# Decode step of a small transformer block: the first twelve granules of each row laid out as closed 512 KiB blocks

## The chip, the cores and the metric

One core of one Trainium2 chip. The metric is the device time of one execution in microseconds, the median over several executions.

## The reference

The block is applied twice, with the same caches: attention of one new token over cached keys and values, then a small ReLU network, each with a residual. Sizes: batch 8, 32 heads of 128, 4096 cached positions, model width 640, hidden width 1728, all bf16.

```python
def _A_ref(x, k_cache, v_cache, wq, wo):            # B=8, Hq=Hkv=32, Sk=4096, Dh=128
    q = (x @ wq).reshape(B, 1, 32, 128).transpose(0, 2, 1, 3)
    p = softmax(einsum("bhqd,bhkd->bhqk", q, k_cache) * 128 ** -0.5)
    o = einsum("bhqk,bhkd->bhqd", p, v_cache)
    return o.transpose(0, 2, 1, 3).reshape(B, 1, 4096) @ wo
def _B_ref(x, w1, w2):
    return relu(x @ w1) @ w2
x = x + _A_ref(layernorm(x), k_cache, v_cache, wq, wo)
x = x + _B_ref(layernorm(x), w1, w2)
x = x + _A_ref(layernorm(x), k_cache, v_cache, wq, wo)
x = x + _B_ref(layernorm(x), w1, w2)
```

The caches are 512 MiB. They don't fit on the core, so most of them is read from DRAM twice, once for each application: of 2 x 1024 blocks of 512 KiB, 1856 are loaded.

## The kernel before

One batch entry is a "row". Its keys and values lie in DRAM as 128 partitions, each with 128 pieces of 4 KiB. Piece `p` of all 128 partitions is a **granule** of 512 KiB, the unit in which buffers are handed out. On the core there are 26 buffers of that size (`arena`). A host routine, `plan`, lays down the whole order of work in advance: it goes through the row for the first layer, then again for the second, with the next row woven in. To spare loads it keeps 24 granules of a row from its first pass to its second: `G - SPARE` = 21 stay in their buffers and three wait elsewhere on the core, mostly in PSUM (`STASH`). While they wait, only five buffers are left to work with. That is the **turn**: the end of a row's first pass and the start of its second.

```python
G = 26                # buffers of one granule
SPARE = 5             # of them free in a turn
STASH = 3
PAD = 2048            # elements after each partition's row: pitch 516 KiB, not 512
...
    first = [(which, hp, g) for which, hp in first for g in range(UNIT)]    # 24 granules
    keep = set(first[: G - SPARE])
    stash = first[G - SPARE : G - SPARE + STASH]
...
    def feed():                       # called whenever a buffer comes free
        while at[0] < len(stream):
            ...                       # most: how long a load may be now, least: how long it must be
            b, p = place(stream[at[0]])
            n = 1
            while n < most and place(stream[at[0] + n]) == (b, p + n):
                n += 1
            ...                       # u: the first of n free buffers in a row, or return
            ops.append(("load", b, p, n, u))
...
    def do_load(b, p, n, u):          # L637 of the profile
        nc.sync.dma_start(out=arena[:, u * GW : (u + n) * GW],
                          in_=A_kv[b, :, p * GW : (p + n) * GW])
...
    # host side
    kv = np.pad(kv.reshape(B, p, -1), ((0, 0), (0, 0), (0, PAD)))
```

A load takes one to eight granules. In the turns, where buffers come free one at a time, it mostly takes one. All loads are issued by SP, in order, and each waits until PE has done with the buffer that it fills.

Of the kernel before, what the change touches and what calls it, by code (L numbers as in the profile page):

```python
# [16 lines left out]
UNIT = 4  # L17
# [5 lines left out]
SOON = 4  # L23
PACE, LATE = 0.6, 2
PAD = 2048
AHEAD = 2
BANK = 512
CAP = 20
# [2 lines left out]
def tile_at(NP, which, hp):  # L31

    return max(0, 2 * hp - 1) if which == "K" else min(2 * hp + 2, 2 * NP - 1)


def plan(B, NP, n_up, n_down):
# [9 lines left out]
    for b in range(B - 1):  # L46
        nxt = [(0, b + 1, hp) for hp in order0]
        cur = [(1, b, hp) for hp in order1]
        if b + 1 < B - 1:
            visits += nxt[:AHEAD] + cur + nxt[AHEAD:]  # L50
        else:
            visits += nxt[:AHEAD] + cur[: NP - AHEAD] + nxt[AHEAD:] + cur[NP - AHEAD :]
    visits += [(1, B - 1, hp) for hp in order1]
    NV = len(visits)
    assert NV == 2 * B * NP and NP % GP == 0
    turns = [visits.index((1, b, order1[0])) for b in range(B)]
    moving = [not any(t - AHEAD - 1 <= i < t + 5 for t in turns) and i < NV - 2 for i in range(NV)]
    last_of = {(layer, b): v for v, (layer, b, hp) in enumerate(visits)}
    direct = [i == NV - 1 or visits[i][0] == 0 and last_of[visits[i][:2]] == i for i in range(NV)]
    ahead = [next((t - i for t in turns if 0 < t - i <= AHEAD), 0) for i in range(NV)]  # L60

# [13 lines left out]
    stream, uses = [], []  # L75
    for which, i in slots:
        layer, b, hp = visits[i]
# [18 lines left out]
    at = [0, 0]  # L96
    clock = [5.0, 6.0]

    def keeps(which, i, g):
        return visits[i][0] == 0 and (which, visits[i][2], g) in keep  # L100
# [6 lines left out]
    def place(x):  # L107

        return visits[x[1]][1], tile_at(NP, x[0], visits[x[1]][2]) * UNIT + x[2]

    def room(n):

        us = [u for u in range(G - n + 1) if not any(owner[u : u + n])]
        return min(us, key=lambda u: max(freed[u : u + n])) if us else None

    def feed():

        while at[0] < len(stream):
            lead = clock[1] - clock[0]
            calm = (PACE * (nth[stream[at[0]]] - at[1]) - LATE - lead) / 1.2  # L120
            least = next((n for us, n in LEADS if lead >= us), 1)
            least = min(least, max(1, (G - len(kept) - 2) // 3))
            most = min(max(least, int(calm)), LEADS[0][1], max(1, (len(stream) - at[0]) // 2))
            least = min(least, most)
            b, p = place(stream[at[0]])
            n = 1
            while n < most and place(stream[at[0] + n]) == (b, p + n):
                n += 1
            least = min(n, least)
            u = next((u for n in range(n, least - 1, -1) if (u := room(n)) is not None), None)  # L130
            if u is None:
                return
            n = next(k for k in range(n, 0, -1) if room(k) == u)
            for k, (which, i, g) in enumerate(stream[at[0] : at[0] + n]):
                ops.extend(("weights",) + w for w in weights.pop(i, []) if which == "K")
                owner[u + k] = True
                where[which, i, g] = u + k
                if keeps(which, i, g):
                    kept[which, b, visits[i][2], g] = u + k
            at[0] += n  # L140
            clock[1] = max(clock[1], clock[0] + 1.4) + 0.1 + 1.2 * n
            lands[u : u + n] = [clock[1] + 2] * n
            ops.append(("load", b, p, n, u))

    def find(which, i, g):
        u = where.get((which, i, g))
        return kept[which, visits[i][1], visits[i][2], g] if u is None else u
# [59 lines left out]
    def finish(layer, b):  # L207

        def own(n, *op):
            return n, ("C", layer, b, *op)  # L210

        c = []
        for k in range(n_up):
            c += [own(15, "up", k)]
            if layer:
                c += [own(0, "relu", k)]
            elif k == min(1, n_up - 1):
                c += [own(0, "var"), own(0, "root")]
        if layer:
            for k in range(n_up):  # L220
                c += [own(15, "down", k)] + [own(0, "var"), own(0, "root")] * (k == n_up // 2)
            return c + [own(0, "add")]
        c += [own(0, "relu")] + [own(14, "down", k) for k in range(n_down)] + [own(0, "add")]
        c += [own(2, "mean"), own(0, "center")] + query(b, 0)
        c += [own(1, "var2"), own(0, "root2")] + query(b, 1)
        return c

    feed()
    for which, i in slots:
        layer, b, hp = visits[i]  # L230
# [16 lines left out]
        for g in range(UNIT):  # L247
            u = find(which, i, g)
# [13 lines left out]
        else:  # L262
# [12 lines left out]
            if last_of[layer, b] == i and (layer == 0 or b == B - 1):  # L275
                chains[-1] += [(14, ("W", i)), (0, ("YC", i))] + finish(layer, b)
            elif layer == 0 or b == B - 1:
                chains[-1] += [(10, ("W", i)), (0, ("Y", i))]
                if last_of[layer, b] == next(v for v in range(i + 1, NV) if visits[v][:2] == (layer, b)):
# [17 lines left out]
def kernel(  # L297
    ctx: ExitStack,
    tc: tile.TileContext,
    A_x: bass.AP,  # L300
    A_kv: bass.AP,
    A_wq: bass.AP,
    A_wo: bass.AP,
# [6 lines left out]
    nc = tc.nc  # L310
    P = nc.NUM_PARTITIONS

    B, Sq, D = A_x.shape
    H = A_wo.shape[1] // D
    NP = H // 2
    Dh = A_kv.shape[1]
    W = (A_kv.shape[2] - PAD) // (2 * NP)
    Sk = W // 2
    Dff = B_w1.shape[1] // (D // P)
    assert Sq == 1 and Dh == P and D % P == 0 and W % (UNIT * P) == 0  # L320
    DC = D // P
    NJ = Sk // P
    GW = W // UNIT
    assert GW == 4 * BANK and Sk == UNIT * 2 * BANK
# [11 lines left out]
    kv = ctx.enter_context(tc.tile_pool(name="kv", bufs=1))  # L336
# [3 lines left out]
    arena = kv.tile([P, G * GW], BF16, name="arena")  # L340
# [25 lines left out]
    def load_weights(which, g=0):  # L366
# [15 lines left out]
        out=ident, in_=ident, pattern=[[-1, P]], compare_op=ALU.not_equal,  # L382
# [12 lines left out]
    for c in range(4):  # L395
        rows, at = slice(32 * c, 32 * c + CJ), c // 2 * 2 * CJ + c % 2
# [237 lines left out]
            copy(out=arena[:, u * GW + n * 2 * BANK : u * GW + (n + 1) * 2 * BANK], in_=t)  # L634

    def do_load(b, p, n, u):
        nc.sync.dma_start(out=arena[:, u * GW : (u + n) * GW], in_=A_kv[b, :, p * GW : (p + n) * GW])  # L637

    def do_q0(g):

# [32 lines left out]
    def do_mm(which, i, g, u):  # L673
# [19 lines left out]
        for c in range(4):  # L693
            if moving[i]:
# [5 lines left out]
                continue  # L700
            s_tiles[i] = o_ps[:, 2 * NJ : 4 * NJ] if ahead[i] == AHEAD else s_ps[:, i % 2 * 2 * NJ : (i % 2 + 1) * 2 * NJ]
            h = 2 * hp + c // 2
# [140 lines left out]
    def do_y(i):  # L843
# [3 lines left out]
        nc.vector.tensor_tensor(out=xT[:, b0 : b0 + nb, :], in0=xT[:, b0 : b0 + nb, :], in1=y, op=ALU.add)  # L847

    does = dict(WS=do_ws, S=do_s, SM=do_sm, SC=do_sc, YC=do_yc, load=do_load, stash=do_stash, unstash=do_unstash, weights=load_weights, mm=do_mm, M1=do_m1, T=do_t, M2=do_m2, B=do_b, E=do_e,
                L=do_l, I=do_i, OC=do_oc, OG=do_og, O=do_o, W=do_w, Y=do_y, C=do_finish, Q0=do_q0, Q=do_q, QC=take_q, QZ=do_qz, PT=do_pt, PC=do_pc, clear=do_clear)  # L850

# [15 lines left out]
def _laid_out(A_x, A_k_cache, A_v_cache, A_wq, A_wo, B_w1, B_w2):  # L867

    p = 128
    B, H, Sk, Dh = A_k_cache.shape  # L870
    D, HD = A_wq.shape
    Dff = B_w1.shape[1]
    NP, NJ, DC, NG, FC = H // 2, Sk // p, D // p, H // 2 // GP, -(-Dff // p)
    c = np.ascontiguousarray
    w2 = np.zeros((FC * p, D), B_w2.dtype)
    w2[:Dff] = B_w2
    k = A_k_cache.reshape(B, NP, 2, UNIT, Sk // UNIT, Dh).transpose(0, 1, 5, 3, 2, 4).reshape(B, NP, Dh, 2 * Sk)
    v = A_v_cache.reshape(B, NP, 2, UNIT, NJ // UNIT, p, Dh).transpose(0, 1, 5, 3, 2, 4, 6).reshape(B, NP, p, -1)
    kv = np.empty((B, p, 2 * NP, 2 * Sk), A_k_cache.dtype)
    for hp in range(NP):  # L880
        kv[:, :, tile_at(NP, "K", hp)] = k[:, hp]
        kv[:, :, tile_at(NP, "V", hp)] = v[:, hp]
    kv = np.pad(kv.reshape(B, p, -1), ((0, 0), (0, 0), (0, PAD)))
    return {
        "A_x": c(A_x),
        "A_kv": kv,
        "A_wq": c(A_wq.reshape(DC, p, NG, HD // NG).transpose(1, 2, 0, 3)).reshape(p, -1),
        "A_wo": c(A_wo.reshape(H, Dh, D).transpose(1, 0, 2)).reshape(Dh, -1),
        "B_w1": c(B_w1.reshape(DC, p, Dff).transpose(1, 0, 2)).reshape(p, -1),
        "B_w2": c(w2.reshape(FC, p, D).transpose(1, 0, 2)).reshape(p, -1),  # L890
    }
# [25 lines left out]
```

## Time and profile before

| | before |
|---|---|
| median of 3 runs | 2340.54 us (2339.28 to 2341.31) |
| profiled span | 2343.0 us |
| load queue, share of 16 DMA engines' span | 99.4% |
| PE busy | 60% |

In the profile, PE is the matrix engine (PEld its weight loads), DVE, ACT and POOL are the other compute engines, and SP is the engine that issues the loads. The page of the kernel before, by slices of the span (each 58.6 us), the count of packets, the load queue, and the chain that ended last by engine:

```profile
...
DMA  9999999999999999999999999999999999999997
GB/s 411 430 433 401 433 432 432 431 396 432 432 432 430 404 434 431 430 427 403 433 432 431 426 412 434 430 432 420 427 431 427 432 416 430 431 431 431 396 433 329
DMA packets 76753, 990.87 MB, mean 423 GB/s; under 512 B 8596, under 2 KB 8596, under 8 KB 36500
...
q1 hardware_dynamic: 76564, 988.12, 99.4%
...
DMA 71%; PE 17%; ACT 6%; DVE 3%; issue 2%; SPq 0%; POOL 0%; ACTq 0%; DVEq 0%; POOLq 0%
...
```

The load queue is busy for 99.4% of what sixteen engines have. The line GB/s is the rate in each slice: it holds near 430 and dips every fifth slice or so, down to 396. Those are the turns. The last line is the chain of waits: 71% of the span passes in waiting for a load. So a change has to pay through the load queue.

The loads of the kernel before, by size, with the median time from issue to landing:

```profile
...
issues: line engine op xcount, KB each, median us to landing
arena<-in_A_kv_dram SPq DMA_DIRECT2D x124, 4096.0 KB, 23.1
arena<-in_A_kv_dram SPq DMA_DIRECT2D x98, 2048.0 KB, 22.7
arena<-in_A_kv_dram SPq DMA_DIRECT2D x218, 512.0 KB, 6.5
...
```

Windows of the kernel before inside the first two turns. The last two columns are the DMA engines' busy share and the rate:

```profile
...
core 0: us, PE busy (x) PEld busy (x) DVE busy (x) ACT busy (x) POOL busy (x), PEclk, DMA share, GB/s
200.00:210.00 10.00, 8.44 (x227) 7.32 (x224) 2.95 (x18) 0.64 (x3) 2.33 (x11) 1.00 0.98 354
480.00:490.00 10.00, 7.76 (x214) 6.22 (x211) 3.19 (x20) 1.22 (x4) 0.56 (x3) 1.00 0.94 363
490.00:500.00 10.00, 8.15 (x177) 6.17 (x175) 1.71 (x10) 1.28 (x6) 1.78 (x8) 1.00 1.00 373
500.00:510.00 10.00, 8.07 (x173) 5.52 (x171) 2.82 (x18) 1.65 (x5) 2.54 (x12) 1.00 1.01 376
...
```

In the turn the engines are nearly as busy as elsewhere (0.94 to 1.01; a share over 1 comes from packets whose records overlap), but move 354 to 376 GB/s where they move about 430 elsewhere. So what they carry there takes longer.

What SP waited for before it issued a load, summed over the span (L637 is the load):

```profile
engine line waited for: us in total, times, longest us
SPq L637 <- DMA arena<-in_A_kv_dram: 836.5, 274, 13.2
SPq L637 <- PE small_ps L781: 301.9, 81, 7.5
SPq L637 <- PE s_ps L695: 290.0, 68, 9.5
SPq L637 <- PE o_ps L687: 261.9, 97, 7.9
SPq L637 <- PE small_ps L742: 101.4, 28, 6.0
...
```

SP waits both for PE, which frees buffers, and for loads, behind which PE stands.

The trace also has a record for each DMA packet, with its size, start and duration. One packet is one partition's run of a load, so a load of one granule has 128 packets of 4 KiB, eight on each engine. From these records of the kernel before I worked out:

```
packet size         4 KiB   8 KiB   16 KiB   32 KiB
packets             27904    6144    12544    15872
median, ns            159     309      611     1213
mean, ns            166.6   310.5    612.3   1215.2
excess per engine    13.3     0.6      1.0      2.2   us   (sum of duration less the median of its size, over 16)
```

(Packets of the load queue alone.) The medians are 150.5 ns per 4 KiB plus 8.5 ns per packet. **Excess** is used below for the last row: the time by which packets outlasted the usual time of their size. Over all sizes of the key and value loads it is 17.5 us. Of these, 13.3 are in the 4 KiB packets, and 10.7 of the 13.3 in the 156 single loads that start in the first twelve granules of a row. It isn't spread evenly: 735 of the 27904 packets of 4 KiB last over 200 ns, 444 ns on average, and these hold 13.1 of the 13.3 us.

### The profile page before, as it was taken

What the parts mean: (1) busy time and instruction counts of PE and PEld (TensorE: products, weight loads), DVE (VectorE), ACT (ScalarE), POOL (GpSimd) and SP (SyncE); (2) the same over time, 40 slices, a digit from 0 to 9 for tenths busy, and PEclk for the clock granted to TensorE, in tenths of its full rate; (3) what the DMA queues carried; (4) which work ended last, traced back from release to release, by engine and by line L of the source; (5) the groups of instructions that cost most, each with busy time, mean ns of one, the idle gap of its engine ahead of it and who ended that gap; (6) DMA issues with size and microseconds to landing.
All of it is one profiled execution on the core that took longest, in us unless ns stands there. A gap on an engine that the chain in (4) does not pass through costs nothing.

```text
span 2343.0 us, 43024 instructions
## 1 busy us (share of the span) xinstructions
PE 1398.6 (60%) x18748; PEld 591.4 (25%) x18748; DVE 496.7 (21%) x2022; ACT 426.3 (18%) x986; POOL 59.5 (3%) x296
## 2 busy tenths in 40 slices
PE   3547654576545764557545675556755567545766
PEld 1214211152111511125111241113411133111523
DVE  1113211131112211122111221112211122111312
ACT  1111211122111221112211121111211112111211
POOL 0000000000000000000000000000000000000000
PEclk9999999999999998555555555555555555555555
DMA  9999999999999999999999999999999999999997
GB/s 411 430 433 401 433 432 432 431 396 432 432 432 430 404 434 431 430 427 403 433 432 431 426 412 434 430 432 420 427 431 427 432 416 430 431 431 431 396 433 329
DMA packets 76753, 990.87 MB, mean 423 GB/s; under 512 B 8596, under 2 KB 8596, under 8 KB 36500
## 3 DMA queue, kind: packets, MB, share of 16 engines
q1 hardware_dynamic: 76564, 988.12, 99.4%
q8 instruction: 146, 2.39, 0.4%
q14 instruction: 43, 0.35, 0.0%
HBM read 988.08 MB, written 0.01 MB: 422 GB/s over the span
## 4 chain that ended last, share of the span: by engine, by line
DMA 71%; PE 17%; ACT 6%; DVE 3%; issue 2%; SPq 0%; POOL 0%; ACTq 0%; DVEq 0%; POOLq 0%
DMA arena<-in_A_kv_dram 71%; PE o_ps L687 5%; PE s_ps L695 4%; PE s_ps L705 2%; ACT P_row L755 2%; ACT o_sb L795 1%; PE small_ps L655 1%; DVE mrow L713 1%; ACT P_sb L761 1%; PE small_ps L800 1%; ACT arena L634 1%; PE small_ps L768 1%; PE small_ps L825 1%; DVE hmx L732 0%; ACT nmax L753 0%
## 5 line engine op out<-in xcount | busy, mean ns | idle before, releaser
L687 PE MATMUL o_ps<-arena,P_sb 128*4 128x512 bf16 x3952 | 584.3, 596 | 402.0 <-DMA arena<-in_A_kv_dram 401.0
L695 PE MATMUL s_ps<-arena,qz 128*4 128x512 bf16 x3040 | 410.3, 602 | 261.1 <-DMA arena<-in_A_kv_dram 249.5
L687 PEld LDWEIGHTS <-P_sb 128*4 128x4 bf16 x3952 | 107.4, 88 | 502.8 <-issue 491.7
L713 DVE TENSOR_REDUCE mrow<-s_ps 100x1 bf16<-100x512 f32 x190 | 131.8, 694 | 323.2 <-PE s_ps L695 323.2
L795 ACT CAST o_sb<-o_ps 100x512 bf16<-100x512 f32 x247 | 144.9, 587 | 289.3 <-PE o_ps L687 286.0
L753 ACT ACTIVATE nmax<-small_ps 100x1 f32<-100x1 f32 x106 | 18.1, 171 | 774.5 <-PE small_ps L742 774.5
L775 DVE CAST P_sb<-small_ps 128x64 bf16<-128x64 f32 x190 | 42.6, 224 | 523.1 <-PE small_ps L768 523.1
L695 PEld LDWEIGHTS <-qz 128*4 128x4 bf16 x3040 | 63.9, 85 | 313.7 <-issue 295.5
L705 PEld LDWEIGHTS <-arena 128*128 128x128 bf16 x4224 | 129.6, 104 | 40.8 <-DMA arena<-in_A_kv_dram 23.4
L705 PE MATMUL s_ps<-qo,arena 128*128 128x1 bf16 x3712 | 123.7, 165 | 17.2 <-ACT P_sb L761 7.6
L768 PE MATMUL small_ps<-few,P_row 100*128 100x16 bf16 x760 | 52.3, 179 | 92.1 <-ACT P_row L755 92.1
L753 ACT ACTIVATE nmax<-small_ps,q_scale 100x1 f32<-100x1 f32 x84 | 22.0, 261 | 398.7 <-PE small_ps L742 398.7
L787 DVE TENSOR_REDUCE lsum<-small_ps 128x2 f32<-128x64 f32 x240 | 53.9, 224 | 171.9 <-PE small_ps L781 171.9
L768 PEld LDWEIGHTS <-P_row 100*128 100x128 bf16 x760 | 35.0, 107 | 186.5 <-ACT P_row L755 178.2
L720 PE MATMUL small_ps<-few,mrow 100*1 100x16 bf16 x190 | 34.4, 181 | 67.6 <-DVE mrow L713 67.6
L755 ACT ACTIVATE P_row<-s_ps,nmax 100x512 bf16<-100x512 f32 x106 | 72.8, 687 | 3.4
L800 PEld LDWEIGHTS <-o_sb 100*128 100x128 bf16 x988 | 45.7, 106 | 107.2 <-ACT o_sb L795 73.8
L655 PE MATMUL small_ps<-xq,wq_sb 128*128 128x1 bf16 x1200 | 48.8, 165 | 38.9 <-DVE qo L812 33.5
L800 PE MATMUL small_ps<-few,o_sb 100*128 100x2 bf16 x988 | 65.1, 170 | 10.7 <-DVE lsum L787 2.2
L727 DVE TENSOR_REDUCE diag<-small_ps 1x2 bf16<-1x16 f32 x190 | 30.8, 162 | 186.9 <-PE small_ps L720 186.9
L720 PEld LDWEIGHTS <-mrow 100*1 100x1 bf16 x190 | 15.0, 79 | 210.8 <-DVE mrow L713 210.8
L755 ACT ACTIVATE P_row<-s_ps,nmax,q_scale 100x512 bf16<-100x512 f32 x84 | 65.3, 778 | 2.8
(225 smaller groups left out, 958.0 us busy)
## 6 DMA issues: line engine op xcount, KB each, us to landing
arena<-in_A_kv_dram SPq DMA_DIRECT2D x124, 4096.0 KB, 23.1
arena<-in_A_kv_dram SPq DMA_DIRECT2D x98, 2048.0 KB, 22.7
arena<-in_A_kv_dram SPq DMA_DIRECT2D x218, 512.0 KB, 6.5
arena<-in_A_kv_dram SPq DMA_DIRECT2D x48, 1024.0 KB, 11.3
arena<-in_A_kv_dram SPq DMA_DIRECT2D x11, 3072.0 KB, 22.4
arena<-in_A_kv_dram SPq DMA_DIRECT2D x11, 2560.0 KB, 20.5
arena<-in_A_kv_dram SPq DMA_DIRECT2D x10, 1536.0 KB, 19.7
wq_sb<-in_A_wq_dram SPq DMA_DIRECT2D x4, 1280.0 KB, 17.6
```

What stands on the lines that cost most here:

```text
L655: nc.tensor.matmul(q_ps[:, h : h + 1], lhsT=wq_sb[:, g, c, (2 * n + h) * Dh : (2 * n + h + 1) * Dh], rhs=xlns[b][:, 0, c : c + 1], start=( ...
L687: nc.tensor.matmul(o_ps[32 * c : 32 * c + CJ, :], lhsT=P_tiles[i][:, h, j : j + CJ], rhs=arena[:, at + c * CJ * Dh : at + (c + 1) * CJ * D ...
L695: nc.tensor.matmul(s_ps[32 * c : 32 * c + CJ, :], lhsT=qz[:, i % 3, c // 2, 3 - g : 3 - g + CJ], rhs=arena[:, at + c * BANK : at + (c + 1) ...
L705: nc.tensor.matmul(s_tiles[i][:, j : j + 1], lhsT=arena[:, at + n * P : at + (n + 1) * P], rhs=qo[:, b, h : h + 1], start=True, stop=True,)
L713: nc.vector.tensor_reduce(out=m_tiles[i][:OR, :1], in_=s_ps[:OR], axis=AX.X, op=ALU.max)
L720: nc.tensor.matmul(turn_ps[:1, : 4 * CJ], lhsT=m[:OR, :1], rhs=rsel[:OR], start=True, stop=True)
L755: nc.scalar.activation(out=P_rows[i][:OR], in_=s_ps[:OR], func=ACT.Exp, bias=nm[:OR, :1], scale=more)
L768: nc.tensor.matmul(P_ps[:, k * 4 * CJ : (k + 1) * 4 * CJ], lhsT=P_row[:OR, k * P : (k + 1) * P], rhs=rsel[:OR], start=True, stop=True,)
L775: nc.vector.tensor_copy(out=P_tiles[i].rearrange("p h (c k) -> p h c k", k=BANK // P), in_=P_ps.rearrange("p (k h c) -> p h c k", k=BANK / ...
L787: nc.vector.tensor_reduce(out=L, in_=(lsum2_ps if ahead[i] else lsum_ps).rearrange("p (h j) -> p h j", h=2), axis=AX.X, op=ALU.add)
L795: nc.scalar.copy(out=o_tiles[i][:OR], in_=o_ps[:OR, :].rearrange("p (j d) -> p j d", j=CJ))
L800: nc.tensor.matmul(oy[i][:, :2], lhsT=o_tiles[i][:OR, j, :], rhs=gsel[:OR, j, :], start=(j == 0), stop=(j == CJ - 1))
```

## The change

The intent: the single loads read 128 pieces of 4 KiB that lie 516 KiB apart. If they were slow for that reason, granules that are closed blocks of DRAM would help. The first twelve granules of each row, where most singles are, move into a tensor of their own, `A_head`. The plan never lets a load cross from the twelfth granule to the next. The rest of each row is twelve pieces shorter, so its pitch becomes 468 KiB.

```diff
+HEAD = 12
...
-            while n < most and place(stream[at[0] + n]) == (b, p + n):
+            while n < most and place(stream[at[0] + n]) == (b, p + n) and p + n != HEAD:
...
     def do_load(b, p, n, u):
-        nc.sync.dma_start(out=arena[:, u * GW : (u + n) * GW], in_=A_kv[b, :, p * GW : (p + n) * GW])
+        if p < HEAD:
+            src, dst = A_head[b, p : p + n].rearrange("n p k -> p n k"), arena[:, u * GW : (u + n) * GW].rearrange("p (n k) -> p n k", n=n)
+            if n == 1:
+                src, dst = A_head[b, p], arena[:, u * GW : (u + 1) * GW]
+            nc.sync.dma_start(out=dst, in_=src)
+        else:
+            nc.sync.dma_start(out=arena[:, u * GW : (u + n) * GW], in_=A_kv[b, :, (p - HEAD) * GW : (p - HEAD + n) * GW])
...
-    kv = np.pad(kv.reshape(B, p, -1), ((0, 0), (0, 0), (0, PAD)))
+    head = kv[:, :, : HEAD * gw].reshape(B, p, HEAD, gw).transpose(0, 2, 1, 3)
+    kv = np.pad(kv[:, :, HEAD * gw :], ((0, 0), (0, 0), (0, PAD)))
```

More of the change, by code (lines that the diff above doesn't have):

```diff
@@ L300 @@
     A_x: bass.AP,
+    A_head: bass.AP,
     A_kv: bass.AP,
@@ L316 @@
     Dh = A_kv.shape[1]
-    W = (A_kv.shape[2] - PAD) // (2 * NP)
+    W = UNIT * A_head.shape[3]
     Sk = W // 2
@@ L882, in _laid_out @@
         kv[:, :, tile_at(NP, "V", hp)] = v[:, hp]
-    kv = np.pad(kv.reshape(B, p, -1), ((0, 0), (0, 0), (0, PAD)))
+    gw = 2 * Sk // UNIT
+    kv = kv.reshape(B, p, -1)
+    head = kv[:, :, : HEAD * gw].reshape(B, p, HEAD, gw).transpose(0, 2, 1, 3)
+    kv = np.pad(kv[:, :, HEAD * gw :], ((0, 0), (0, 0), (0, PAD)))
     return {
         "A_x": c(A_x),
+        "A_head": c(head),
         "A_kv": kv,
```

## The prediction

> **What bounds the kernel now.** The DMA stream. The page gives the load queue 99.4% of sixteen engines' span (423 GB/s on average), and the chain of waits is 71% "DMA arena<-in_A_kv_dram"; PE is busy 60%. In the long middle of a row the windows show 428 to 436 GB/s. The rate drops where one row's second pass gives way to the next (the "turns"): windows at 200:210 and 480:510 us give 354, 363, 373 and 376 GB/s, with a DMA share of 0.94 to 1.00 and PE busy 7.8 to 8.4 of 10 us.
>
> **What the dips are made of.** The packet records show one packet for one partition's run. Medians: 4 KiB 159 ns, 8 KiB 309, 16 KiB 611, 32 KiB 1213: about 150.5 ns for 4 KiB and 8.5 ns per packet of any size. The 27904 packets of 4 KiB (218 single loads) have a mean of 167 ns; what they take over the median is 13.3 us per engine, against 4.2 us for all larger packets. Loads that start in the first twelve granules are 156 singles, 18 doubles and two larger ones (counted from the plan of before). Of the 13.3 us, 10.7 lie in those 156.
>
> **What the change does.** It moves 192 of 1856 granules (10%) to rows 4 KiB apart instead of 516 KiB. The singles' packets stay 4 KiB, so the 8.5 ns are not saved. The 36 granules of the larger loads break into 4 KiB packets: +4608 of these, about +1.1 us per engine. Eight loads that cross granule 12 are split: eight more issues, some +0.6 us. The rest of a row gets a pitch of 468 KiB, also an odd multiple of 4 KiB, so I expect the bulk to stay.
>
> **How much can be won.** At most the 10.7 us, if the long packets come from the DRAM addresses. The Trainium skill ("DMA: Bandwidth & Descriptors", Latency and other measured facts) says that row pitches of large powers of two are slow, and that 4 KiB of padding or contiguous tiles restore the rate. The pitch of before is padded already. I doubt that addresses are the cause: the excess goes with late issue. Single loads whose first packet starts 2.0 to 2.5 us after the issue have 0.20 us of excess each; at 2.5 to 3.5 us 0.06; at 4.0 to 5.0 us 0.01. Late issues wait for a buffer that PE frees (the queue's own waits: over 900 us on PE and DVE), and the layout doesn't touch that. I take a fifth of 10.7 us as won, -2.1, some -0.6 for better reads of contiguous rows, and +1.7 of cost: -1 us.
>
> **Prediction:** 2339.5 us, 2330 to 2349. Faster by over 2%: 1%. Within 2%: 96%. Slower: 3%.
>
> **What would show it.** 32 KiB packets stay at 1213 ns. 4 KiB packets grow by about 4600 and keep a median of 159 ns. If late issue is the cause, their mean stays above 164 ns and the turns' windows under 400 GB/s. If addresses were, the mean falls to 160 or 161 ns, the turns rise above 405 GB/s, and the time falls by 7 to 10 us.
>
> **What would make it wrong.** Contiguous reads that are widened over several rows, so that the 8.5 ns go too (up to 10 us more won); [...] a pitch of 468 KiB that slows the bulk (1% is 21 us).

## The result, and the profile after

| | before | after |
|---|---|---|
| median of 6 runs | 2340.63 us (2338.52 to 2343.6) | 2341.94 us (2341.12 to 2343.17) |
| profiled span | 2343.0 us | 2340.2 us |

The ratio is 1.0006, with a 95% interval of 0.9993 to 1.0019: the same. Ratios here and below are the mean time of one kernel's fast runs over that of the other's in the same rounds, so not quite the ratio of the medians quoted.

The page of the changed kernel, the same lines:

```profile
...
DMA  9999999999999999999999999999999999999997
GB/s 411 427 433 404 434 430 432 429 402 431 434 433 428 409 434 432 434 425 413 432 433 431 421 414 431 430 433 418 426 432 430 431 414 427 433 432 430 399 433 332
DMA packets 79377, 990.87 MB, mean 423 GB/s; under 512 B 8660, under 2 KB 8660, under 8 KB 40916
...
q1 hardware_dynamic: 79188, 988.12, 99.5%
...
DMA 71%; PE 18%; ACT 5%; DVE 4%; issue 2%; SPq 0%; POOL 0%; DVEq 0%; ACTq 0%; POOLq 0%
...
```

The dips stand where they stood (404, 402, 409 against 401, 396, 404). There are 4416 more packets under 8 KiB: 4352 of 4 KiB, because loads of several granules in the head are now cut at every granule (29 granules, 3712 packets) and five more loads are single (640), and 64 small ones, which I put down to the four more loads (525 against 521, sixteen each).

The loads of the changed kernel, by source and size:

```profile
...
issues: line engine op xcount, KB each, median us to landing
arena<-in_A_kv_dram SPq DMA_DIRECT2D x123, 4096.0 KB, 23.1
...
arena<-in_A_head_dram SPq DMA_DIRECT2D x163, 512.0 KB, 6.5
...
arena<-in_A_kv_dram SPq DMA_DIRECT2D x60, 512.0 KB, 6.4
...
arena<-in_A_head_dram SPq DMA_DIRECT2D x11, 1024.0 KB, 8.7
...
```

163 single loads and eleven doubles come from the closed blocks, besides one load of three granules and one of four. A single load from there takes 6.5 us to land, as it did before.

The windows of the first two turns in the changed kernel:

```profile
...
core 0: us, PE busy (x) PEld busy (x) DVE busy (x) ACT busy (x) POOL busy (x), PEclk, DMA share, GB/s
200.00:210.00 10.00, 8.66 (x235) 7.55 (x233) 3.17 (x19) 0.64 (x3) 2.31 (x11) 1.00 0.96 351
480.00:490.00 10.00, 7.49 (x233) 6.77 (x230) 3.21 (x20) 0.59 (x1) 1.21 (x7) 1.00 0.98 383
490.00:500.00 10.00, 8.24 (x163) 5.89 (x160) 2.01 (x11) 1.28 (x6) 1.10 (x5) 1.00 0.98 385
500.00:510.00 10.00, 7.86 (x170) 5.50 (x167) 2.98 (x19) 1.65 (x5) 2.52 (x12) 1.00 1.00 367
...
```

351, 383, 385 and 367 GB/s, against 354, 363, 373 and 376. The turns are as slow as they were.

What SP waited for in the changed kernel (L643 is a load from the closed blocks, L645 one from the rest):

```profile
engine line waited for: us in total, times, longest us
SPq L645 <- DMA arena<-in_A_kv_dram: 695.5, 172, 14.8
SPq L645 <- PE small_ps L789: 468.4, 101, 7.0
SPq L645 <- PE s_ps L703: 251.0, 65, 8.0
SPq L645 <- PE o_ps L695: 162.0, 70, 6.7
SPq L645 <- PE small_ps L750: 102.7, 26, 6.2
SPq L643 <- DMA arena<-in_A_head_dram: 61.1, 49, 8.1
...
```

SP still waits for PE and for the loads on which PE depends. The packet records: the 4 KiB packets keep their median of 159 ns and have a mean of 164.7, an excess of 11.4 us per engine over 32256 packets; the 32 KiB packets stay at 1213 ns. Is 11.4 against 13.3 a gain? The first control below says no.

### The profile page after: what moved, and what is told of

Its sections match the earlier page's. It is cut to its first block, busy times and chain, and to the rows that moved or that the text cites. A ratio compares the mean times of both kernels' runs of the same rounds, so it can differ in the third digit from the quotient of the medians.

```text
span 2340.2 us, 43040 instructions
## 1 busy us (share of the span) xinstructions
PE 1392.4 (59%) x18748; PEld 595.4 (25%) x18748; DVE 496.7 (21%) x2022; ACT 426.1 (18%) x986; POOL 59.0 (3%) x296
## 3 DMA queue, kind: packets, MB, share of 16 engines
q1 hardware_dynamic: 79188, 988.12, 99.5%
## 4 chain that ended last, share of the span: by engine, by line
DMA 71%; PE 18%; ACT 5%; DVE 4%; issue 2%; SPq 0%; POOL 0%; DVEq 0%; ACTq 0%; POOLq 0%
DMA arena<-in_A_kv_dram 65%; DMA arena<-in_A_head_dram 6%; PE s_ps L703 5%; PE o_ps L695 4%; PE s_ps L713 2%; ACT P_row L763 2%; DVE mrow L721 1%; PE small_ps L663 1%; PE small_ps L808 1%; ACT o_sb L803 1%; ACT P_sb L769 1%; PE small_ps L776 1%; PE small_ps L833 1%; ACT arena L636 1%; ACT nmax L761 1%
## 5 line engine op out<-in xcount | busy, mean ns | idle before, releaser
L713 PEld LDWEIGHTS <-arena 128*128 128x128 bf16 x4224 | 129.5, 104 | 42.8 <-issue 17.6
L713 PE MATMUL s_ps<-qo,arena 128*128 128x1 bf16 x3712 | 123.7, 165 | 18.4 <-ACT P_sb L769 7.6
L820 DVE TENSOR_TENSOR oT<-small_ps,invL 128x2 bf16<-128x2 f32 x120 | 19.1, 159 | 290.1 <-PE small_ps L808 289.3
```

Of the source, the lines that this page charges most:

```text
L713: nc.tensor.matmul(s_tiles[i][:, j : j + 1], lhsT=arena[:, at + n * P : at + (n + 1) * P], rhs=qo[:, b, h : h + 1], start=True, stop=True,)
```

## The experiments

Two theories. **Late issue:** packets outlast their usual time when a load is issued too shortly before its turn in the queue, which happens when buffers are few; addresses have no part in it. **Addresses:** the rows 516 KiB apart make the packets of single loads long, and the change cured that, but gave the gain back by its new plan, its added packets or its new pitch.

### How far two profiles of one kernel differ

The kernel before, once more, without an edit (one run, state unknown; it ran after the next four experiments, together with those that change the number of buffers).

> The kernel before, once more, to see how far two profiles of the same kernel differ. If the excess of the 4 KiB packets (13.3 us in the first profile) comes out between 9 and 15 us, the differences of one or two microseconds between the profiles of the earlier runs mean nothing.

2338.99 us, span 2337.2 us. The excess of the 4 KiB packets was 9.4 us, their mean 164.4 ns. So the same kernel gave 13.3 and 9.4 us, and the changed kernel's 11.4 lies between. The spread from one execution to the next is of this kind too: of the eight profiles of kernels with five buffers in a turn, the two with the most excess over all sizes (18.9 and 17.5 us) have the longest spans (2344.8 and 2343.0 us), and the two with the least (13.6 and 13.7) the shortest (2337.2 and 2337.3).

### The layout alone

The plan, the pitch and all loads but the head's singles as before; those come from `A_head`, which holds a second copy.

```diff
     def do_load(b, p, n, u):
+        if p < HEAD and n == 1:
+            nc.sync.dma_start(out=arena[:, u * GW : (u + 1) * GW], in_=A_head[b, p])
+            return
         nc.sync.dma_start(...)
```

> Only the single loads of the head come from the tensor of closed granules; the plan, every other load and the row pitch of 516 KiB are as before. Late-issue theory: the excess of the 4 KiB packets over their median stays above 10 us per engine (13.3 in before), their mean at 164 to 168 ns, and the time within 3 us of before. Address theory: the 10.7 us of excess in the head's singles fall under 2 us, the mean of the 4 KiB packets to about 161 ns, and the time falls by 6 to 10 us.

2343.66 us against 2341.18, ratio 1.0008 (0.9994 to 1.0022). The excess of the 4 KiB packets was 13.4 us, their mean 166.7 ns; in the head's 156 singles it was 11.1 us, where the two profiles of before have 10.7 and 7.7. The address theory wanted under 2 us. It fails here already, without any of the things that could have given a gain back.

### The new plan alone

```diff
-            while n < most and place(stream[at[0] + n]) == (b, p + n):
+            while n < most and place(stream[at[0] + n]) == (b, p + n) and p + n != HEAD:
```

> The plan of the change (loads that end at granule 12 of a row) with the layout of before. Late-issue theory: within 3 us of before, excess of the 4 KiB packets 11 to 15 us. Theory that the layout wins and the new plan gives it back: 5 to 10 us slower than before.

2341.17 us against 2341.18, ratio 1.0003 (0.999 to 1.0016), excess of the 4 KiB packets 11.1 us. The plan costs nothing that these runs resolve.

### The whole change with the old pitch

```diff
-PAD = 2048
+PAD = 13 * 2048
```

> The whole change, with the rest of each row padded to the pitch of before (516 KiB instead of 468). Late-issue theory: equal to the changed kernel within 2 us. Theory that the layout wins and the new pitch gives it back: 5 to 10 us faster than the changed kernel, with less excess in the 16 and 32 KiB packets (3.3 us together in after).

2341.16 us, ratio to before 1.0002 (0.999 to 1.0015); the changed kernel had 1.0006 in its own rounds. The 16 and 32 KiB packets have an excess of 3.5 us together, against 3.3 in the changed kernel. The new pitch took nothing back.

### The loads by themselves

All compute is taken out (the results are wrong; one run). Ten stages of 96 single loads each; the ring of buffers gets smaller from pair to pair, and within a pair the first stage reads rows 516 KiB apart, the second closed blocks.

```python
STAGES = ((24, 0), (24, 1), (5, 0), (5, 1), (4, 0), (4, 1), (3, 0), (3, 1), (2, 0), (2, 1))
for depth, layout in STAGES:
    for k in range(B * HEAD):
        (together if layout else strided)(k // HEAD, k % HEAD, k % depth)
```

> Wrong results on purpose. No compute: ten stages of 96 single loads of the head each, in a ring of 24, 5, 4, 3 and 2 buffers, each depth once from rows 516 KiB apart and once from closed granules. A load waits only for the one that filled its buffer before. Late-issue theory: at depth 24 both layouts have a mean of 159 to 161 ns a packet; as the ring shrinks to 3 and 2, packets get longer or gaps open, by the same amount in both layouts. Address theory: at depth 24 the strided stage is longer than the closed one by 4% or more (mean 165 ns or more against 160), and the same at every depth.

Windows of this kernel, one for each stage, in the order of the stages (the columns before the last three are engines that do nothing here):

```profile
...
core 0: us, DVE busy (x) POOL busy (x), PEclk, DMA share, GB/s
5.90:126.20 120.30, 0.00 (x0) 0.00 (x0) 1.00 1.03 420
126.10:246.00 119.90, 0.00 (x0) 0.00 (x0) 1.00 1.03 420
245.90:366.70 120.80, 0.00 (x0) 0.00 (x0) 1.00 1.02 417
368.10:489.00 120.90, 0.00 (x0) 0.00 (x0) 1.00 1.02 416
490.30:611.60 121.30, 0.00 (x0) 0.00 (x0) 1.00 1.02 415
611.50:731.50 120.00, 0.00 (x0) 0.00 (x0) 1.00 1.03 420
731.30:888.40 157.10, 0.00 (x0) 0.00 (x0) 1.00 0.93 322
887.60:1046.90 159.30, 0.00 (x0) 0.00 (x0) 1.00 0.91 317
1046.10:1257.50 211.40, 0.00 (x0) 0.00 (x0) 1.00 0.79 239
1257.20:1463.30 206.10, 0.00 (x0) 0.00 (x0) 1.00 0.78 244
...
```

Read in pairs. With 24, 5 and 4 buffers both layouts give 415 to 420 GB/s. With three, 322 and 317; with two, 239 and 244. Within a pair the rates differ by 2.1% at most, now one way and now the other; the number of buffers costs up to 43%. Single loads reach 420 GB/s even with 24 buffers, where larger loads make the kernel's 430 and more: that part of the dip in the turns belongs to the size of the loads, and is not excess. From the packet and issue records of the same run:

```
buffers                               24            5             4             3             2
layout                          apart closed  apart closed  apart closed  apart closed  apart closed
mean packet, ns                 159.1  159.0  159.0  159.5  160.3  159.0  187.2  187.3  216.7  209.2
excess per load, us              0.00   0.00   0.00   0.00   0.01   0.00   0.23   0.23   0.46   0.40
issue to first packet, med. us   7.94   7.97   3.70   4.05   2.77   2.80   2.12   2.17   1.25   1.22
issue to landing, median us      9.97   9.97   6.22   6.22   4.98   4.98   4.82   4.90   4.43   4.29
```

A load issued 2.1 us before its first packet has 0.23 us of excess. In the kernel before, single loads issued 2.0 to 2.5 us early had 0.20 us each (0.14 in the second profile). So a short ring makes an excess of the size seen in the turns, without PE, without a turn, and with closed blocks as well as with rows apart.

The excess is made of a few long packets here too: with two buffers 15 to 17% of the packets last over 200 ns, some 500 ns on average, and hold 99% of the excess; 59 to 71% of it lies in the first and the last sixteen packets of each load, in order of start.

But the lead (the time from issue to first packet) does not fix the excess by itself: between 2.75 and 3.0 us the single loads of the kernel before have 0.05 us each (42 loads, and 49 in the second profile), and the 134 of the ring of four 0.00 (the first eight of each stage left out). Half of the kernel's 13.3 us (6.6) lies at leads of 2.5 to 3.5 us.

At three and two buffers the engines also stand idle at times (busy shares 0.91 to 0.93 and 0.78 to 0.79). At full rate one load passes every 1.25 us (120 us for 96). With two buffers a load takes 4.29 to 4.43 us to land, or 3.4 to 3.5 times as long: so three buffers can't keep the queue full and four just can, as the windows show, before PE has held a buffer for any time at all. (The 4.98 us with four buffers are no evidence for this: at full rate, four loads in flight take four times 1.25 us, as five take 6.22 us.) The kernel has five in a turn.

### Three buffers in a turn, with either layout

The two buffers taken from the turn hold two granules that were stashed before, so the stream keeps its 1856 granules. First in the kernel before, then in the changed one:

```diff
-SPARE = 5
+SPARE = 3
```

> The kernel before with three free buffers in a turn instead of five (two more granules are kept instead of held in PSUM; the stream has the same 1856 granules). Late-issue theory: the loads of the turns are issued later before their turn, the excess of the 4 KiB packets rises above 25 us, gaps open, and the time rises by 15 to 60 us, with the addresses of before. Address theory: the same addresses in the same number, so no change over 5 us.

> The changed kernel with three free buffers in a turn. Late-issue theory: the same rise as in e5_three_buffers within 6 us, although every granule of the head is closed. Address theory: closed granules keep their packets short, so much less of a rise than in e5.

2416.4 us against 2342.86 with the old layout, ratio 1.0313 (1.0296 to 1.033); 2416.23 us with the closed blocks, ratio 1.0315 (1.03 to 1.0331). The rise of some 73 us is above the 15 to 60 expected: I had the idle time too small. The excess of the 4 KiB packets is 42.8 us with rows apart and 40.1 us with closed blocks, where the address theory wanted short packets. In the records of e5, 119 of 227 single loads have their first packet within 2.5 us of the issue (22 of 218 in before). The excess over all sizes is 46.7 us per engine (17.5 and 13.6 in the two profiles of before), and the engines are idle for 51 us between the first load and the last, against 8 and 6. The two rises are 29 to 33 and 43 to 45 us, which together account for the rise.

Windows of the first turn, three buffers, rows apart:

```profile
...
200.00:210.00 10.00, 6.29 (x190) 5.76 (x188) 2.20 (x14) 0.64 (x3) 2.31 (x11) 1.00 0.78 253
210.00:220.00 10.00, 6.49 (x114) 4.16 (x111) 2.12 (x11) 1.20 (x4) 0.00 (x0) 1.00 0.87 305
...
```

The same windows, three buffers, closed blocks:

```profile
...
200.00:210.00 10.00, 6.73 (x201) 6.22 (x197) 2.21 (x14) 0.64 (x3) 2.31 (x11) 1.00 0.81 264
210.00:220.00 10.00, 5.64 (x93) 3.52 (x93) 1.95 (x10) 1.00 (x4) 0.00 (x0) 1.00 0.84 277
...
```

The columns before the clock are the busy times of PE, its weight loads, DVE, ACT and POOL. DMA share and rate fall together, to 253 and 305 GB/s with rows apart and to 264 and 277 with closed blocks. This experiment had the largest effect for the layout to show up in, and it doesn't show.

### Seven buffers in a turn

```diff
-SPARE = 5
+SPARE = 7
```

> The kernel before with seven free buffers in a turn; 16 more granules are loaded (1872), which at 1.215 us each costs 19 us. Late-issue theory: with two buffers more the loads of the turns are issued over 3.5 us early, the excess of the 4 KiB packets falls from 13.3 to under 5 us with the addresses of before, and the time rises by 8 to 14 us instead of 19. Address theory: the excess stays near its share (194 singles instead of 218, 11 to 12 us) and the time rises by about 18 us.

2356.02 us against 2342.86, ratio 1.0058 (1.0043 to 1.0073): a rise of 13.2 us for 16 more granules, with the addresses of before. The excess of the 4 KiB packets fell to 5.4 us, just short of the "under 5" expected. Not all loads were issued over 3.5 us early either: 24 of 194 singles were not, against 125 of 218 in before. Part of it only moved: the larger packets have 8.9 us of excess, where they had 4.2 in both profiles of before. By the records, the packets' usual time rose by 18.4 us, and the idle time between the first load and the last fell from 8 and 6 us to 4; the total excess of 14.3 us lies within what before showed. So of the 18.4 us some 5 came back, mostly as less idle time, and this version beats neither kernel.

### Do addresses matter at all?

The padding of the rows is taken away, so that they lie exactly 512 KiB apart:

```diff
-PAD = 2048
+PAD = 0
```

> The kernel before with the padding of the rows taken away: the pitch is 512 KiB instead of 516. It asks whether addresses can matter here at all. If they can [...], packets of all sizes get longer than 159 and 1213 ns and the time rises by 1 to 4% (2365 to 2435 us). If the time stays within 5 us, the pitch costs a load of this kernel nothing, padded or not.

2340.93 us against 2341.0, ratio 0.9998 (0.9982 to 1.0015). The medians stay at 159 and 1213 ns, and the excess of the 4 KiB packets is 11.0 us. The Trainium skill ("DMA: Bandwidth & Descriptors", Latency and other measured facts) has 207 GB/s at this pitch for copies between HBM tensors, 3% below the 214 that it gives for a pitch of 4 MiB padded by 4 KiB and calls full rate; for the loads of this kernel no difference shows.

The same, with the head's singles from closed blocks as in the layout-alone experiment:

> As e8_no_pad, but the single loads of the head come from closed granules. If e8 is slower, the head's singles (156 of 1856 granules) lose their share of the slowdown here, so that e9 is faster than e8 by some 8% of what e8 lost, plus what the turns lost to late releases. If e8 equals before, e9 equals it too, within 3 us.

2341.62 us, ratio 1.0002 (0.9987 to 1.0017), excess of the 4 KiB packets 9.6 us. Equal, as it must be if the pitch costs nothing.

Last, the loads alone with a pitch of 512 KiB and the order within each pair turned round:

> Wrong results on purpose: the loads alone again, without the padding, and the closed granules first at each depth (24, 4, 3, 2), so that the order of the stages is not what makes them equal. Late-issue theory: closed at depth 24 has a mean of 159 ns, and at depths 3 and 2 means of about 187 and 213 ns in the closed stage too. Strided at 512 KiB: 159 to 161 ns at depth 24 if this pitch costs nothing, 165 ns or more if it does.

One run. Mean packets, closed then apart: 159.1 and 159.0 ns with 24 buffers, 160.0 and 160.3 with four, 185.1 and 188.8 with three, 203.3 and 203.1 with two. The layouts differ by 2% at most, so it is neither the order of the stages nor the pitch that makes them equal. The two-buffer means came out some 5% under the 213 that I had expected.

## Why the prediction was right or wrong

- **The time: right.** 2341.94 us lies in 2330 to 2349, and the ratio was within 2%. The point 2339.5 is 2.4 us low.
- **What bounds the kernel: right.** The load queue has 99.5% of sixteen engines' span after the change as well, and dips in the same places.
- **Late issue as the cause of the long packets: right in part.** Shown is that the number of buffers makes the long packets and the layout doesn't: the loads alone make such an excess out of nothing but a short ring, in both layouts; three buffers in a turn make it over three times as large in both layouts; seven bring that of the 4 KiB packets down to 5.4 us; the layout alone leaves it at 13.4 us. Not shown is that the lead is what counts: a smaller ring shortens the lead and lowers the number of loads in flight at once, and no run separates the two. At the same lead of 2.75 to 3.0 us the kernel has more excess than the ring of four (0.05 against 0.00 us a load), so something besides the lead takes part in the turns. Open, too, is why a few packets last some 450 ns, rather than all packets lasting 159 ns and starting later: no run here separates the parts of a packet's time.
- **"I take a fifth of 10.7 us as won, -2.1": wrong.** Nothing was won: 11.1 us of excess in the head's singles with the layout alone, 10.7 and 7.7 in two profiles of before. My hedge of a fifth had no ground in the trace. That the time came out right doesn't depend on it: the three terms that I summed lie between -2.1 and +1.7 us, inside the spread of the runs.
- **"Some -0.6 for better reads of contiguous rows": not seen.** With a full ring the mean packet is 159.1 ns apart and 159.0 ns closed.
- **"+1.7 of cost": about the size, in the part that can be read.** In the records, the usual time of all packets rose by 1.4 us per engine (2270.8 to 2272.2), the price of 4352 more packets of 4 KiB and fewer of other sizes. The loads grew by four, not eight, because the plan also merged others differently. The ratio of 1.0006 is 1.4 us as well, but its interval goes from -1.6 to +4.4 us, so the agreement is not proof.
- **The bulk at a pitch of 468 KiB: right.** 1213 ns for 32 KiB before and after, and the old pitch changes nothing (1.0002).
- **The marks I set: one was weak.** The mean stayed above 164 ns (164.7) and the turns under 400 GB/s, as late issue wanted. But a second profile of before has 164.4, and one of the whole change with the old pitch 163.7, so 164 was no safe line. The address theory's 160 or 161 stayed far off.

## What to carry to other kernels

When a queue is busy all the time but slow, look at how many transfers are in flight, and how long before its first packet each was issued, before looking at its addresses. Here too few buffers came with longer packets, and that looked like slow memory in every average. To tell the two apart, run the transfers alone in rings of decreasing size, with both layouts; it takes one run. And the Trainium skill's advice to issue early and wait late ("DMA: Bandwidth & Descriptors", Rules for kernel authors) can be given a count. An estimate from the loads alone: the time from issue to landing in a short ring (4.3 to 4.4 us with two buffers), plus the time that the consumer holds a buffer, over the time of one transfer at full rate (1.25 us). That is four for the transfers alone. How long PE holds a buffer was not measured; in the kernel five left 9 to 13 us of excess in the 4 KiB packets, and three cost 3%.

## What the Trainium skill lacked or had wrong

- "DMA: Bandwidth & Descriptors", Latency and other measured facts: copies between HBM tensors with a row pitch of 512 KiB are given as 207 GB/s, against 214 at a pitch of 4 MiB padded by 4 KiB. For loads to the core's buffers nothing of it shows: whole kernel 0.9998 (0.9982 to 1.0015) without padding, and 159.0 ns per 4 KiB packet in the loads alone. The page says that its figures are for copies; it has no such figure for loads.
- The same page, Anatomy of one DMA, fits 2.0 us plus bytes over 436 GB/s for a transfer issued from GpSimd; for 512 KiB that is an estimate of 3.2 us. Transfers of that size issued from SP, with one other in flight, took 4.3 to 4.4 us in the median with two buffers (3.4 us at the least in one run of the loads alone, 3.0 in the other). The page has no such fit for transfers from SP.
- Of the pages on DMA, HBM, SBUF and traces, none says how many transfers have to be in flight for full rate. Here, of 512 KiB each: four gave 415 to 420 GB/s, three 317 to 322, two 239 to 244.
- Nor does one say that too few transfers in flight show as longer packets: mean 185 to 189 ns with three and 203 to 217 with two, for packets of 159 ns, in a record that counts as busy time.
